# Six wide products per weight block, the softmax epsilon folded into z, and one sum of exponentials per token tile

## The chip, the cores and the metric

The kernel runs on one core of one Trainium2 chip. A core has five engines that run side by side and meet only at semaphores: TensorE (PE) multiplies matrices, VectorE (DVE), ScalarE (ACT) and GpSimd (POOL) work element by element, and SyncE (SP) issues most DMAs. Matrix products land in PSUM, which has eight banks; everything else that is on the chip lies in SBUF. The metric is the device time of one execution in microseconds, lower is better; a profiled execution gives the span and what each engine did in it.

## What is computed

A pre-norm linear attention block followed by a token-mixing MLP, on 2048 tokens of width 512, with 32 heads of 16 and a hidden width of 1792 over the tokens. Cut to what matters:

```python
pq = einsum("bhsd,hdf->bhsf", q, w_phi); pk = einsum("bhsd,hdf->bhsf", k, w_phi)
phi_q = concat([softmax(pq), softmax(-pq)], -1)      # over the 16 features of a head
phi_k = concat([softmax(pk), softmax(-pk)], -1)
kv  = einsum("bhsf,bhsd->bhfd", phi_k, v)
z   = einsum("bhsf->bhf", phi_k)
den = einsum("bhqf,bhf->bhq", phi_q, z)[..., None] + 1e-6
o   = einsum("bhqf,bhfd->bhqd", phi_q, kv) / den
h   = x + concat_heads(o) @ wo                        # x: the input; q, k, v from layernorm(x)
# token mixing, on g = layernorm(layernorm(h))
u   = gelu(einsum("bsd,sf->bdf", g, w1) + b1)         # sums over the tokens
out = h + transpose(einsum("bdf,fs->bds", u, w2) + b2)
```

## The kernel before

All products run on PE in 32-bit form with operands split into a high and a low part: hi x hi, hi x lo and lo x hi are added up in PSUM, three matmuls for one product (`mm3`, or its like with other names).

**Attention.** The 2048 tokens are 16 tiles of 128. K, V and Q are projected tile by tile; the exponentials of a Q tile, for both signs, lie in the tile `eq` (128 x 1024: 64 groups of 16). For the quotient each tile needs the sums of its exponentials for both signs (`smq`, in PSUM, by `q_sum`, line 229), the same sums weighted with z (`ez` = `eq` * `zB` on POOL, line 456, then a sum on DVE into `tz`, line 465), and from both the factor `w` (lines 466 to 471), by which POOL scales `eq` (line 474). The softmax sums of the two signs stand crosswise: `q_sum` writes the sum of sign c to place 1 - c, so that `tz`, multiplied with it, brings the two signs to a common denominator. Line 466 adds the 1e-6 of the reference. `zB`, z summed over all tokens and broadcast to all rows, comes from PE and is copied out by ACT (line 503). From line 432 on the order of PE, DVE, ACT and POOL is that of the code; a loop over `it` (line 716) runs the steps of different tiles side by side, and `turns` (line 175) deals out two lists of DVE operations alternately. Before line 432 a scheduler orders the engines by its own estimates. The normalized tiles `hs` get their low part from POOL (line 62), and the first matrix products of the MLP (`fill`, `pu`) read them.

**The last stage.** `out` is made of eight blocks `sp` of 256 tokens. Each sums over seven slices `p` of the hidden width; a block is a 2 x 2 matrix product computed with seven products of half size instead of eight (operand sums `wraw`, split into `whi` and `wlo`, for the weights; `un` and `uf` for the hidden values). A product takes one of two forms: *wide* (line 1106) is one matmul of 512 columns, hi weights times the high and the low half of the values side by side, and one of 256 columns, lo weights times the high half; the two halves of its PSUM bank are added by the engine that reads it. *narrow* (line 1110) is three matmuls of 256 columns that all add into half a bank, so that two narrow products share a bank. The table `PROD` gives for each product its operands, its bank and, where it is narrow, its half; of the seven, five are wide and two narrow, on six banks. The last block uses the table `LAST`, narrow products alone on four banks. Banks are handed out in turn from all eight, so a block begins on banks that the block before it has not used and goes on to banks that it has.

At the end of a block, its last two slices run product by product, so that banks fill one after the other, and DVE and ACT read them (lines 1162 to 1181): ACT copies one half of bank 0 and the second halves of three banks (`low`), DVE forms the sums `e`, `u2`, `u3` and the outputs `ot`, and POOL issues DMAs that add `ot` and `low` to `out`. Between these, DVE also prepares weights for later steps: for each group of two steps `sums_w2` (lines 857 to 859), `hi_w2` on ACT (line 992) and `lo_w2` (line 1002). Seven slices per block and two per group make blocks alternate: after blocks with an even number a group's `lo`, `hi` and `sums` come within the reading of the banks; in blocks with an odd number `lo`, `hi` and `sums` come at slice 5, ahead of it.

Of the kernel before, what the change touches and what calls it, by code (L numbers as in the profile page):

```python
# [9 lines left out]
F32 = mybir.dt.float32  # L10
# [7 lines left out]
P = 128  # L18
# [6 lines left out]
GRP = 2  # L25
# [5 lines left out]
V_NOT = (0, 1, 11)  # L31
SUMS = 8
LAG = 5
WARM = 9
# [4 lines left out]
def block_kernel(ctx: ExitStack, tc: tile.TileContext, x, xT, wT, phic, wo, w1, b1, w2, b2,  # L39
# [17 lines left out]
    nc.vector.memset(eps2, EPS * EPS)  # L57

# [88 lines left out]
    def signs(e):  # L147
        return e.rearrange("p g (a c h d) -> p (g a) c h d", a=2, c=2, h=2)
# [75 lines left out]
    def q_sum(t):  # L224

        assert t < SUMS or t - SUMS in W, "a tile's sums would go where others are still wanted"
        SQ[t] = sums[:, t % SUMS]
        e = signs(EQ[t])
        return [lambda c=c: nc.vector.reduce_sum(SQ[t][:, :, 1 - c], e[:, :, c], axis=AX.X) for c in range(2)]

# [227 lines left out]
    def s_den(t):  # L458


        tz = az.tile([P, NPR, 2, 2], F32, name="tz")
        den = az.tile([P, NPR, 2], F32, name="den")
        W[t] = az.tile([P, NPR, 2, 2], F32, name="w", bufs=3)
        other = SQ[t]
        return [lambda: nc.vector.reduce_sum(tz.rearrange("p g c h -> p (g c h)"), heads(EZ[t]), axis=AX.X),
                lambda: nc.vector.scalar_tensor_tensor(tz[:, :, 0], other[:, :, 1], 1e-6, tz[:, :, 0],
                                                       op0=ALU.mult, op1=ALU.add),
                lambda: nc.vector.tensor_mul(tz, other, tz),
                lambda: nc.vector.reduce_sum(den, tz.rearrange("p g c h -> p g h c"), axis=AX.X),
                lambda: nc.vector.reciprocal(den, den),  # L470
                lambda: nc.vector.tensor_mul(W[t], other, den.unsqueeze(2).to_broadcast([P, NPR, 2, 2]))]  # L471
# [28 lines left out]
    for g in range(2):  # L500
        pz = ps_k.tile([P, 4, P], F32, name="pk_ps")
        nc.tensor.matmul(pz, ones, zacc[:, 4 * g:4 * g + 4, :], start=True, stop=True)
        nc.scalar.activation(zB[:, 4 * g:4 * g + 4, :], pz, AF.Copy)  # L503
    q_exp(0)
# [94 lines left out]
    def s_moments(t):  # L599

        junk = ak.tile([P, D], F32, name="hj", bufs=1)
        if t == 0:
            ak.tile([P, 104], F32, name="end", bufs=1)
        nc.scalar.activation(VE[t][:, 1:2], VE[t][:, 2:3], AF.Copy, scale=-1.0 / D)
        nc.scalar.activation(junk, HT[t], AF.Square, bias=VE[t][:, 1:2], accum_out=VE[t][:, 3:4])
        nc.scalar.activation(VE[t][:, 0:1], VE[t][:, 3:4], AF.Identity, scale=(1.0 + EPS) / D, bias=eps2)
        if t >= NT - 2:
            nc.scalar.dma_start(out[t * P:(t + 1) * P, :], HT[t])
# [476 lines left out]
    for p in range(NEAR, NP):  # L1085
# [45 lines left out]
    for n, (sp, p) in enumerate(STEPS):  # L1131
        t = 2 * sp
        last = t + 2 == NT
        if n % GRP == 0 and p < NP - 1:
            lo_w2()
            hi_w2()
            sums_w2()
        if p == 0:
            bank = []
            for _ in range(6):  # L1140
                pool = (ps_f, ps_q, ps_b, ps_b)[n_bank % 8 // 2]
                bank.append(pool.tile([P, 2, HD], F32, name="py", tag="pu"))
# [16 lines left out]
        if not last:  # L1159
# [3 lines left out]
            for i in range(3):  # L1163
                nc.scalar.activation(low[:, i], bank[3 + i][:, 1], AF.Copy)
            nc.vector.tensor_add(e[:, 1], bank[0][:, 1], e[:, 1])
            nc.vector.tensor_sub(u2, bank[1][:, 0], e[:, 1])
            nc.vector.tensor_add(u2, bank[1][:, 1], u2)
            nc.vector.tensor_sub(u3, u2, bank[2][:, 0])
            nc.vector.scalar_tensor_tensor(e[:, 0], bank[2][:, 1], -1.0, u2, op0=ALU.mult, op1=ALU.subtract)

            def out_block(i, h, o, add):
                nc.vector.scalar_tensor_tensor(ot[:, i, h], o, b2s[:, t + i:t + i + 1], add, op0=ALU.add, op1=ALU.add)  # L1172

            out_block(0, 0, bank[2][:, 1], u3)
            out_block(0, 1, bank[3][:, 0], u3)
# [79 lines left out]
```

## Time and profile before

| what | value |
|---|---|
| median of 3 runs | 518.52 us (518.47 to 518.72) |
| the profiled execution, its own time | 518.56 us |
| its span | 516.8 us |
| PE busy | 510.9 us (99%), 3595 matmuls |
| DVE / ACT / POOL busy | 445.5 / 296.8 / 245.0 us |
| granted TensorE clock | 1.00 |

The span runs from the first to the last instruction; the 1.8 us between it and the execution's own time lie around it. A busy engine here means that an instruction of it was under way. Matmuls overlap their neighbours, so the cost of one is read from the distance of starts in a run of them and not from its own duration. The list of waits puts idle time of an engine to the instruction that ended it; the chain is followed back from the last instruction to whatever released each step.

### The profile page before, as it was taken

How to read it: one execution, taken by the hardware profiler on the slowest of the kernel's cores; microseconds unless marked ns; L12 is line 12 of the kernel's file. 1: busy time of each engine (PE TensorE's matmuls, PEld its weight loads, DVE VectorE, ACT ScalarE, POOL GpSimd, SP SyncE). 2: the span in 40 equal slices, each digit the busy share in tenths (PEclk: the TensorE clock that was granted, in tenths of full speed). 3: DMA queues.
4: the chain of work that ended last, by engine and by line, in shares of the span. 5: the costliest groups of instructions: out<-in, count | busy, mean ns of one | idle time of the engine just before them, and what ended most of it. 6: DMA issues, size and time to landing. Idle time of an engine off the chain costs nothing.

```text
span 516.8 us, 9476 instructions
## 1 busy us (share of the span) xinstructions
PE 510.9 (99%) x3595; PEld 442.9 (86%) x3595; DVE 445.5 (86%) x789; ACT 296.8 (57%) x494; POOL 245.0 (47%) x188
## 2 busy tenths in 40 slices
PE   9999999999999999999999999999999999999997
PEld 8888888887877778777788899998889999899997
DVE  6893999986799998777796998989989898988985
ACT  6998944434255876668976643457653434434430
POOL 2479799975999999985343200000002212212220
PEclk9999999999999999999999999999999999999999
DMA  8744310000041324334322233374135787677843
GB/s 313 270 127 122 81 53 29 1 1 3 12 154 41 103 84 140 124 124 122 115 89 83 82 105 104 99 245 141 43 123 117 162 192 171 119 162 159 191 50 77
DMA packets 36300, 58.56 MB, mean 113 GB/s; under 512 B 3744, under 2 KB 19360, under 8 KB 36256
## 3 DMA queue, kind: packets, MB, share of 16 engines
q1 hardware_dynamic: 31648, 50.85, 31.3%
q0 software_dynamic: 4032, 6.42, 9.9%
q8 instruction: 28, 0.46, 0.4%
q10 hardware_dynamic: 576, 0.69, 0.4%
q14 instruction: 16, 0.13, 0.1%
HBM read 46.81 MB, written 11.14 MB: 112 GB/s over the span
## 4 chain that ended last, share of the span: by engine, by line
PE 89%; POOL 7%; DVE 2%; ACT 1%; issue 1%; POOLq 0%
PE py L1106 17%; PE pu L936 12%; PE py L1110 10%; PE pu L66 7%; PE pu L67 7%; PE pu L68 7%; PE pv L67 3%; PE pv L68 3%; PE pv L66 3%; PE pk_ps L66 2%; PE pk_ps L68 2%; PE pk_ps L67 2%; POOL ez L456 2%; POOL eq L474 2%; PE po L68 2%; PE tn L548 2%
## 5 line engine op out<-in xcount | busy, mean ns | idle before, releaser
L1176 POOL DMA_DIRECT2D out<-ot x7 | 6.2, 884 | 142.1 <-DVE ot L1172 142.1
L992 ACT ACTIVATE whi<-wraw 128x1792 fp32r<-128x1792 f32 x28 | 47.6, 1701 | 44.1 <-DVE wraw L859 20.3
L1002 DVE TENSOR_TENSOR wlo<-wraw,whi 128x1792 fp32r<-128x1792 f32 x28 | 56.6, 2021 | 8.4 <-PE py L1110 6.9
L67 PE MATMUL pu<-hs,whi 128*128 128x512 f32 x128 | 50.3, 393 | 1.2 <-POOL hs L62 1.2
L66 PE MATMUL pu<-hs,whi 128*128 128x512 f32 x128 | 50.1, 399 | 0.0
L1106 PE MATMUL py<-uf,whi 128*128 128x512 f32 x175 | 48.4, 393 | 0.0
L68 PE MATMUL pu<-hs,wlo 128*128 128x512 f32 x128 | 48.0, 390 | 0.0
L897 ACT ACTIVATE whi<-wraw 128x896 fp32r<-128x896 f32 x24 | 22.9, 954 | 31.2 <-PE pu L936 26.4
L456 POOL TENSOR_TENSOR ez<-eq,zB 128x1024 f32<-128x1024 f32 x16 | 38.3, 2399 | 4.4 <-ACT zB L503 4.4
L1110 PE MATMUL py<-uf,whi 128*128 128x256 f32 x210 | 39.0, 283 | 0.0
L936 PE MATMUL pu<-ht,whi 128*128 128x256 f32 x192 | 35.6, 283 | 0.0
L208 POOL TENSOR_TENSOR pk<-pk,sk 128x1024 f32<-128x1024 f32 x16 | 30.9, 1938 | 7.3 <-DVE sk L207 7.2
L62 POOL TENSOR_TENSOR hs<-hb,hs 128x512 fp32r<-128x512 f32 x16 | 22.4, 1400 | 23.9 <-ACT hs L61 23.8
L550 ACT ACTIVATE pht<-tn 128x512 f32<-128x512 f32 x32 | 17.4, 595 | 28.4 <-PE tn L548 28.3
L474 POOL TENSOR_TENSOR eq<-eq,w 128x1024 f32<-128x1024 f32 x16 | 32.4, 2028 | 1.3 <-DVE w L471 1.2
L1110 PEld LDWEIGHTS py<-uf,whi 128*128 128x128 f32 x210 | 32.7, 192 | 0.0
L1106 PEld LDWEIGHTS py<-uf,whi 128*128 128x128 f32 x175 | 29.8, 189 | 3.5
L212 POOL TENSOR_TENSOR zacc<-zacc,pk 128x1024 f32<-128x1024 f32 x13 | 31.2, 2399 | 0.5
L1106 PEld LDWEIGHTS py<-uf,wlo 128*128 128x128 f32 x175 | 27.9, 190 | 4.0
L66 PEld LDWEIGHTS pu<-hs,whi 128*128 128x128 f32 x128 | 24.1, 188 | 7.2 <-issue 2.5
L936 PEld LDWEIGHTS pu<-ht,whi 128*128 128x128 f32 x192 | 30.0, 192 | 0.0
L1110 PE MATMUL py<-uf,wlo 128*128 128x256 f32 x105 | 29.7, 283 | 0.0
(207 smaller groups left out, 1625.0 us busy)
## 6 DMA issues: line engine op xcount, KB each, us to landing
wraw<-in_w SPq DMA_DIRECT2D x28, 512.0 KB, 4.5
wraw<-in_w SPq DMA_DIRECT2D x48, 256.0 KB, 2.8
xraw<-in_xT SPq DMA_DIRECT2D x16, 256.0 KB, 3.1
xh<-in_x SPq DMA_DIRECT2D x16, 256.0 KB, 2.7
h<-in_x SPq DMA_DIRECT2D x16, 256.0 KB, 2.7
out<-h SPq DMA_DIRECT2D x14, 256.0 KB, 2.7
out<-ot POOLq DMA_DIRECT2D x14, 256.0 KB, 4.8
wraw<-in_wT SPq DMA_DIRECT2D x12, 256.0 KB, 4.6
```

The source lines that it names most:

```text
L66: nc.tensor.matmul(o, ah, bh, start=first, stop=False)
L67: nc.tensor.matmul(o, ah, bl, start=False, stop=False)
L68: nc.tensor.matmul(o, al, bh, start=False, stop=last)
L208: nc.gpsimd.tensor_mul(heads(PK[t]), heads(PK[t]), sk.unsqueeze(2).to_broadcast([P, 2 * H, DH]))
L212: nc.gpsimd.tensor_add(zacc, zacc, PK[t])
L456: nc.gpsimd.tensor_mul(EZ[t], EQ[t], zB)
L474: nc.gpsimd.tensor_mul(heads(EQ[t]), heads(EQ[t]), W[t].rearrange("p g c h -> p (g c h)").unsqueeze(2).to_broadcast([P, 2 * H, DH]))
L936: nc.tensor.matmul(ACC[p][bk][:, half], WS[p, i][x][:, a], hb[b][y], start=i == 0 and half == 0 and k == 0, stop=i == NT // 2 - 1 and k == ...
L992: nc.scalar.activation(WH[g], RAW[g], AF.Copy)
L1002: nc.vector.tensor_sub(wl_, RAW[g], WH[g])
L1106: nc.tensor.matmul(o, w, u, start=p == 0 and not low, stop=p == NP - 1, skip_group_check=True)
L1110: nc.tensor.matmul(bank[bk][:, half], AW[sp, p][x][:, a], UB[p, b][:, y], start=p == 0 and half == 0 and i == 0, stop=p == NP - 1 and i == ...
```

## The change

Three things are edited. First, the sums of a tile's exponentials are one DVE reduction over all 64 groups of 16, in their own order, in place of two over 32 groups each; where `w` and the denominator are formed, the result is read with the axis of the signs turned (`[:, :, ::-1]`). Second, line 466 goes: half of 1e-6 is added to each entry of `zB` when ACT copies it out, by an Identity with a bias tile in place of a Copy; summed against the exponentials and multiplied crosswise, the two halves make the same 1e-6. Third, product (0, 0) becomes wide and gets a bank of its own; seven banks are used by blocks 0 to 6 and four by the last. DVE reads one more half bank per block. In the first block the product on the seventh bank is left for slices 0 and 1 together. The sums that odd blocks formed at slice 5 move behind the reading of the banks; after even blocks `lo` and `hi` move behind the last output, but for block 6, where they keep their place.

```diff
+DEN_EPS = 1e-6
...
-    eps2 = cst.tile([P, 1], F32, name="eps2")
+    eps2 = cst.tile([P, 2], F32, name="eps2")
...
-    nc.vector.memset(eps2, EPS * EPS)
+    nc.vector.memset(eps2[:, :1], EPS * EPS)
+    nc.vector.memset(eps2[:, 1:], DEN_EPS / 2)
...
         SQ[t] = sums[:, t % SUMS]
-        e = signs(EQ[t])
-        return [lambda c=c: nc.vector.reduce_sum(SQ[t][:, :, 1 - c], e[:, :, c], axis=AX.X) for c in range(2)]
+        return [lambda: nc.vector.reduce_sum(SQ[t].rearrange("p g c h -> p (g c h)"), heads(EQ[t]), axis=AX.X)]
...
-        other = SQ[t]
+        other = SQ[t][:, :, ::-1]
         return [lambda: nc.vector.reduce_sum(tz.rearrange("p g c h -> p (g c h)"), heads(EZ[t]), axis=AX.X),
-                lambda: nc.vector.scalar_tensor_tensor(tz[:, :, 0], other[:, :, 1], 1e-6, tz[:, :, 0],
-                                                       op0=ALU.mult, op1=ALU.add),
                 lambda: nc.vector.tensor_mul(tz, other, tz),
...
-        nc.scalar.activation(zB[:, 4 * g:4 * g + 4, :], pz, AF.Copy)
+        nc.scalar.activation(zB[:, 4 * g:4 * g + 4, :], pz, AF.Identity, bias=eps2[:, 1:])
...
-    PROD = ((2, 1, 0, None), (5, 5, 1, None), (0, 0, 2, 0), (1, 4, 2, 1), (3, 6, 3, None), (6, 2, 4, None),
-            (4, 3, 5, None))
+    PROD = ((2, 1, 0, None), (5, 5, 1, None), (0, 0, 2, None), (1, 4, 3, 0), (3, 6, 4, None), (6, 2, 5, None),
+            (4, 3, 6, None))
...
         if n % GRP == 0 and p < NP - 1:
             lo_w2()
             hi_w2()
-            sums_w2()
+            if p < NP - 2 or last:
+                sums_w2()
         if p == 0:
             bank = []
-            for _ in range(6):
+            for _ in range(4 if last else 7):
...
         if p == 0:
-            products(sp, [p], order)
+            products(sp, [p], order[:-1] if n == 0 else order)
+            continue
+        if n == 1:
+            steps(sp, [p], order[:-1])
+            products(sp, [0, p], order[-1:])
             continue
...
             nc.vector.tensor_sub(u3, u2, bank[2][:, 0])
-            nc.vector.scalar_tensor_tensor(e[:, 0], bank[2][:, 1], -1.0, u2, op0=ALU.mult, op1=ALU.subtract)
+            nc.vector.tensor_sub(u3, u3, bank[2][:, 1])
+            nc.vector.scalar_tensor_tensor(e[:, 0], bank[3][:, 0], -1.0, u2, op0=ALU.mult, op1=ALU.subtract)
...
             nc.gpsimd.dma_start(out[t * P:(t + 1) * P, :], flat(ot[:, 0]), accum_op=ALU.add)
-            if n % GRP == 0:
+            ahead = t + 4 == NT
+            if ahead:
                 lo_w2()
                 hi_w2()
-            out_block(1, 0, bank[4][:, 0], e[:, 0])
-            out_block(1, 1, bank[5][:, 0], e[:, 1])
+            out_block(1, 0, bank[5][:, 0], e[:, 0])
+            out_block(1, 1, bank[6][:, 0], e[:, 1])
+            if n % GRP == 0 and not ahead:
+                lo_w2()
+                hi_w2()
...
-            if n % GRP == 0:
-                sums_w2()
+            sums_w2()
             continue
```

On PE, in slices 2 and 3 of block 1, where a run of wide matmuls (line 1106, in the new kernel 1105) meets the narrow ones (1110, now 1109), there stood before (a name with a number is one buffer of its kind):

```order
L1106 MATMUL py<-uf,whi 128x512 x10
L1106 MATMUL py<-uf,wlo_4674 128x256 x5
L1110 MATMUL py<-uf,whi 128x256 x2
L1110 MATMUL py<-uf,wlo_4674 128x256
L1110 MATMUL py<-uf,whi 128x256 x2
L1110 MATMUL py<-uf,wlo_4674 128x256
L1106 MATMUL py<-uf,wlo_4674 128x256 x5
```

And now, at the same place on PE:

```order
L1105 MATMUL py<-uf,whi 128x512 x12
L1105 MATMUL py<-uf,wlo_4638 128x256 x6
L1109 MATMUL py<-uf,whi 128x256 x2
L1109 MATMUL py<-uf,wlo_4638 128x256
L1105 MATMUL py<-uf,wlo_4638 128x256 x6
```

One group of three narrow matmuls per slice is gone, and one 512-column and one 256-column matmul per slice have come in its place.

On DVE, at the end of block 1 (an odd one), the reading of the banks stood between these rows before; `u` with a number is `u2` or `u3`:

```order
L1002 TENSOR_TENSOR wlo_4756<-wraw,whi 128x1792
L857 TENSOR_TENSOR wraw<-wraw 128x512
L858 TENSOR_TENSOR wraw<-wraw 128x256
L859 TENSOR_TENSOR wraw<-wraw 128x256
L1165 TENSOR_TENSOR e<-py,e 128x256
L1166 TENSOR_TENSOR u_4798<-py,e 128x256
L1167 TENSOR_TENSOR u_4798<-py,u_4798 128x256
L1168 TENSOR_TENSOR u_4799<-u_4798,py 128x256
L1169 SCALAR_TENSOR_TENSOR e<-py,u_4798 128x256
L1172 SCALAR_TENSOR_TENSOR ot<-py,b2s,u_4799 128x256 x2
L1172 SCALAR_TENSOR_TENSOR ot<-py,b2s,e 128x256 x2
L1002 TENSOR_TENSOR wlo<-wraw_4719,whi 128x1792
```

And now (lines shifted by one to five):

```order
L1001 TENSOR_TENSOR wlo_4716<-wraw,whi 128x1792
L1169 TENSOR_TENSOR e<-py,e 128x256
L1170 TENSOR_TENSOR u_4751<-py,e 128x256
L1171 TENSOR_TENSOR u_4751<-py,u_4751 128x256
L1172 TENSOR_TENSOR u_4752<-u_4751,py 128x256
L1173 TENSOR_TENSOR u_4752<-u_4752,py 128x256
L1174 SCALAR_TENSOR_TENSOR e<-py,u_4751 128x256
L1177 SCALAR_TENSOR_TENSOR ot<-py,b2s,u_4752 128x256 x2
L1177 SCALAR_TENSOR_TENSOR ot<-py,b2s,e 128x256 x2
L856 TENSOR_TENSOR wraw<-wraw 128x512
L857 TENSOR_TENSOR wraw<-wraw 128x256
L858 TENSOR_TENSOR wraw<-wraw 128x256
```

The three operations of `sums_w2` moved from ahead of the nine reading operations to behind them, and these have become ten.

On DVE, in pass 1 of the loop over `it`, where the logits and sums of one tile are dealt out against the denominator of another, there stood before:

```order
L164 TENSOR_REDUCE mx<-pu 128x32
L465 TENSOR_REDUCE tz<-ez 128x64
L165 TENSOR_REDUCE mn<-pu 128x32
L466 SCALAR_TENSOR_TENSOR tz<-smq,tz 128x16x2
L158 TENSOR_TENSOR eq<-pu,mx 128x16x32
L468 TENSOR_TENSOR tz<-smq,tz 128x64
L229 TENSOR_REDUCE smq<-eq 128x16x2
L469 TENSOR_REDUCE den<-tz 128x32
L229 TENSOR_REDUCE smq<-eq 128x16x2
L470 RECIPROCAL den<-den 128x32
L471 TENSOR_TENSOR w<-smq,den 128x64
```

And now:

```order
L166 TENSOR_REDUCE mx<-pu 128x32
L466 TENSOR_REDUCE tz<-ez 128x64
L167 TENSOR_REDUCE mn<-pu 128x32
L467 TENSOR_TENSOR tz<-smq,tz 128x64
L160 TENSOR_TENSOR eq<-pu,mx 128x16x32
L468 TENSOR_REDUCE den<-tz 128x32
L230 TENSOR_REDUCE smq<-eq 128x64
L469 RECIPROCAL den<-den 128x32
L470 TENSOR_TENSOR w<-smq,den 128x64
```

Two operations fewer stand ahead of `w`, and the sum of exponentials is one of double length that stands before the reciprocal.

More of the change, by code (lines that the diff above doesn't have):

```diff
@@ L605, in s_moments @@
         nc.scalar.activation(junk, HT[t], AF.Square, bias=VE[t][:, 1:2], accum_out=VE[t][:, 3:4])
-        nc.scalar.activation(VE[t][:, 0:1], VE[t][:, 3:4], AF.Identity, scale=(1.0 + EPS) / D, bias=eps2)
+        nc.scalar.activation(VE[t][:, 0:1], VE[t][:, 3:4], AF.Identity, scale=(1.0 + EPS) / D, bias=eps2[:, :1])
         if t >= NT - 2:
@@ L1163, in block_kernel @@
             for i in range(3):
-                nc.scalar.activation(low[:, i], bank[3 + i][:, 1], AF.Copy)
+                nc.scalar.activation(low[:, i], bank[4 + i][:, 1], AF.Copy)
             nc.vector.tensor_add(e[:, 1], bank[0][:, 1], e[:, 1])
@@ L1168, in block_kernel @@
             nc.vector.tensor_sub(u3, u2, bank[2][:, 0])
-            nc.vector.scalar_tensor_tensor(e[:, 0], bank[2][:, 1], -1.0, u2, op0=ALU.mult, op1=ALU.subtract)
+            nc.vector.tensor_sub(u3, u3, bank[2][:, 1])
+            nc.vector.scalar_tensor_tensor(e[:, 0], bank[3][:, 0], -1.0, u2, op0=ALU.mult, op1=ALU.subtract)
             def out_block(i, h, o, add):
                 nc.vector.scalar_tensor_tensor(ot[:, i, h], o, b2s[:, t + i:t + i + 1], add, op0=ALU.add, op1=ALU.add)
-            out_block(0, 0, bank[2][:, 1], u3)
-            out_block(0, 1, bank[3][:, 0], u3)
+            out_block(0, 0, bank[3][:, 0], u3)
+            out_block(0, 1, bank[4][:, 0], u3)
             nc.gpsimd.dma_start(out[t * P:(t + 1) * P, :], flat(ot[:, 0]), accum_op=ALU.add)
-            if n % GRP == 0:
+            ahead = t + 4 == NT
+            if ahead:
                 lo_w2()
                 hi_w2()
-            out_block(1, 0, bank[4][:, 0], e[:, 0])
-            out_block(1, 1, bank[5][:, 0], e[:, 1])
+            out_block(1, 0, bank[5][:, 0], e[:, 0])
[3 more added lines that the diff above has]
+                hi_w2()
             nc.gpsimd.dma_start(out[(t + 1) * P:(t + 2) * P, :], flat(ot[:, 1]), accum_op=ALU.add)
```

## The prediction

> **What bounds the kernel.** I read the busy times first, then what PE waits for, then the chain, and then the order of time at three places: the ends of blocks, the attention loop and the start of the last stage. First the page's row of PE, PE's waits (engine, line, releaser: us in total, times, longest), and two stretches of the windows view:
>
> ```profile
> PE 510.9 (99%) x3595; PEld 442.9 (86%) x3595; DVE 445.5 (86%) x789; ACT 296.8 (57%) x494; POOL 245.0 (47%) x188
> ...
> PE pu L67 <- POOL hs L62: 1.2, 1, 1.2
> PE pk_ps L301 <- DVE eps L57: 1.1, 1, 1.1
> PE pk_ps L137 <- ACT wkh L293: 0.2, 1, 0.2
> ...
> 64.00:128.00 64.00, 64.00 (x518) 52.29 (x517) 58.26 (x92) 26.75 (x35) 54.13 (x31) 1.00 0.06 18
> 320.00:380.00 60.00, 60.00 (x407) 55.67 (x406) 55.68 (x120) 34.75 (x52) 0.00 (x0) 1.00 0.42 132
> ```
>
> PE is a wall. In 516.8 us it shows three waits, and only one in the body of the program: 1.2 us for POOL. So the change can gain what it takes out of PE's own queue plus at most that wait, and it can lose wherever PE newly waits. The rows of a kernel whose DVE is busy 86% invite one to count DVE operations; those are worth nothing here unless PE was waiting for them.
>
> **What a product costs on PE.** From the chain in order of time (start, us, what) and the timeline of PE (start, us, then idle time if any); the rows from 399.67 on are a run of two slices:
>
> ```profile
> 388.91 1.44 PE py L1110 x12
> 407.59 2.78 PE py L1106 x16
> 475.15 1.44 PE py L1110 x12
> 495.94 17.64 PE py L1110 x147
> ...
> 399.67 2.46 PE L1106 MATMUL py<-uf,whi 128*128 128x512 f32 x10
> 401.96 0.76 PE L1106 MATMUL py<-uf,wlo 128*128 128x256 f32 x5
> 402.56 0.40 PE L1110 MATMUL py<-uf,whi 128*128 128x256 f32 x2
> ...
> 409.52 0.40 PE L1106 MATMUL py<-un,whi 128*128 128x512 f32 x1
> 411.64 0.40 PE L1106 MATMUL py<-un,whi 128*128 128x512 f32 x1
> ```
>
> The last block, narrow products alone, takes 17.64 us for 147 matmuls: 0.120 us each, so a narrow product is 3 x 0.120 = 0.360 us. Ten matmuls of 512 columns take 401.96 - 399.67 = 2.29 us, 0.229 each, and five of 256 columns 402.56 - 401.96 = 0.60, again 0.120: a wide product is 0.349 us. Run product by product, eight wide ones (x16) take 2.78 us, 0.3475 each. The columns are the same, 768; one instruction fewer saves 0.011 to 0.0125 us. These prices make a block 7 x (5 x 0.349 + 2 x 0.360) = 17.26 us, and the same twelve matmuls come back every (475.15 - 388.91) / 5 = 17.25 us, so nothing else lies in a block. The exchange is made in 7 blocks x 7 slices = 49 products: 0.54 to 0.61 us; I take **0.55 us**.
>
> The Trainium skill, "TensorE: Matmul & The Clock Gate", section "Back-to-back issue gap", gives an isolated matmul N/2.4 ns plus a fixed 2.5 ns at full clock. By that, one matmul fewer would be worth 2.5 ns, 49 of them 0.12 us, and the time 518.4. The trace disagrees: its 256-column matmul stands 120 ns apart where the rule has 109, and the measurement decides.
>
> **The banks.** Seven of eight banks per block leave one free one for the next block. Let T be the first matmul of the next block, 409.52. By the prices above, bank 0 of the ending block is complete at T - 4.2, banks 1 to 5 at T - 3.5, - 2.8, - 2.1, - 1.4, - 0.7, bank 6 at T. The next block needs old bank 0 at T + 0.35, 1 at 0.70, 2 at 1.05, 3 at 1.40, 4 at 1.75, 5 at 2.10. Before, its sixth product needs old bank 3 at 411.64. DVE and ACT at this (odd) end, and DVE at the even end after it:
>
> ```profile
> 406.34 0.36 ACT L1162 ACTIVATE e<-py 128x256 f32<-128x256 f32 x1
> ...
> 404.87 2.03 DVE L1002 TENSOR_TENSOR wlo<-wraw,whi 128x1792 fp32r<-128x1792 f32 x1 [1.26 <-PE py L1110]
> 408.33 0.42 DVE L1165 TENSOR_TENSOR e<-py,e 128x256 f32<-128x256 f32 x1
> 409.84 0.42 DVE L1168 TENSOR_TENSOR u<-u,py 128x256 f32<-128x256 f32 x1
> 410.52 0.87 DVE L1172 SCALAR_TENSOR_TENSOR ot<-py,b2s,u 128x256 f32<-128x256 f32 x2
> 411.30 0.87 DVE L1172 SCALAR_TENSOR_TENSOR ot<-py,b2s,e 128x256 f32<-128x256 f32 x2
> ...
> 423.17 0.42 DVE L1165 TENSOR_TENSOR e<-py,e 128x256 f32<-128x256 f32 x1
> 426.87 2.03 DVE L1002 TENSOR_TENSOR wlo<-wraw,whi 128x1792 fp32r<-128x1792 f32 x1 [0.38 <-PE py L1106]
> ```
>
> Before, the pair of outputs at 410.52 ends at 411.39 and frees bank 3 a quarter of a microsecond ahead of its use at 411.64. That was the tightest hand-over, and PE did not wait. Now the sums have left their place, and DVE can begin right behind `wlo`, at 406.8, T - 2.7 (the copy by ACT is done at 406.70). At the pitch of the rows (408.33 to 409.84 for three operations), the new subtraction 0.46 behind L1168, bank 0 is free at T - 2.3, 1 at - 1.3, 2 at - 0.3, 3 at + 0.4, 4 at + 0.8, 5 at + 1.2: the least margin is 0.9 us. At even ends DVE begins at 423.17, T - 3.6, and all six are free by T + 0.4. So **no wait for banks: 0**, and the tenth reading operation (0.42 us, the row of L1168) lies under PE. If that cover were gone, it would cost 0.42 us at an end.
>
> What is late instead: behind odd ends the sums now start at about T + 1.6, and the next `lo` ends about T + 5.1 (before, sums and `lo` were done by T + 4.6). PE's first lo matmul on it stands in slice 2: two slices (4.89) and twelve 512-column matmuls (2.75) behind T, at T + 7.6, a margin of 2.5 us. Behind even ends `lo` ends at T + 2.6, needed at slice 1's end of hi matmuls, T + 5.2. At block 6 `lo` keeps its place and waits for PE as at 426.87. In the POOL queue, after even ends, the second `ot` DMA now stands ahead of the first `low`; nothing on PE reads `out`.
>
> **The start of the last stage.** Bank 6 of block 0 is a bank that the last hidden slice has just filled, read by the activation:
>
> ```profile
> 377.26 1.37 ACT L800 ACTIVATE u<-pu,b1s 128x512 f32<-128x512 f32 x2 [4.72 <-PE pu L68]
> ...
> 377.74 1.07 PE L1106 MATMUL py<-un,whi 128*128 128x512 f32 x4
> ```
>
> It is the first of the two tiles, read by 377.95. PE reaches the product on it after what is left of slice 1, two hi, six small wide and three narrow matmuls, 1.4 us behind 377.74: 0. The scheduler also reorders some matmuls before 126 us and among the fills around 365 us; the windows above have PE at 64.00 of 64 and 60.00 of 60, with its inputs ready: 0, bounded at 0.3 either way, about PE's one short wait in such a place (0.2).
>
> **The attention loop.** DVE's groups (x count, busy, mean ns), then DVE, POOL and PE in order of time:
>
> ```profile
> L229 DVE TENSOR_REDUCE smq<-eq 128x32 f32<-128x512 f32 x32 | 21.9, 683 | 0.2
> L465 DVE TENSOR_REDUCE tz<-ez 128x64 f32<-128x1024 f32 x16 | 19.3, 1209 | 3.9 <-POOL ez L456 3.9
> L466 DVE SCALAR_TENSOR_TENSOR tz<-smq,tz 128x32 f32<-128x32 f32 x16 | 3.0, 187 | 0.3
> ...
> 185.66 1.38 DVE L665 TENSOR_TENSOR wlo<-wraw,whi 128x512 fp32r<-128x512 f32 x1
> 191.28 2.22 DVE L665 TENSOR_TENSOR wlo<-wraw,whi 128x512 fp32r<-128x512 f32 x1
> ...
> 164.70 0.55 POOL L611 TENSOR_TENSOR r<-ve,mhalf 128x1 f32<-128x1 f32 x1 [0.67 <-ACT ve L606]
> 166.56 2.39 POOL L474 TENSOR_TENSOR eq<-eq,w 128x1024 f32<-128x1024 f32 x1
> 174.38 2.39 POOL L474 TENSOR_TENSOR eq<-eq,w 128x1024 f32<-128x1024 f32 x1
> 179.09 1.29 POOL L62 TENSOR_TENSOR hs<-hb,hs 128x512 fp32r<-128x512 f32 x1
> 182.20 1.94 POOL L474 TENSOR_TENSOR eq<-eq,w 128x1024 f32<-128x1024 f32 x1
> 184.10 2.40 POOL L456 TENSOR_TENSOR ez<-eq,zB 128x1024 f32<-128x1024 f32 x1
> 186.44 1.74 POOL L62 TENSOR_TENSOR hs<-hb,hs 128x512 fp32r<-128x512 f32 x1
> ...
> 188.23 0.50 PE pu L67
> ```
>
> No row has a sum of 1024 values into PSUM; L465 has the input, L229 the output, and between them it costs 1.21 to 1.37 us; I take 1.21, since length sets these. A tile then saves 2 x 0.683 - 1.209 + 0.187 = 0.34 us of DVE. A read with the signs turned has no row; the nearest is L466, which takes every other pair of the same PSUM tile in 0.187. I add nothing; were the two such reads of a tile each slower by that much, 0.37, the tile would come out even. Sixteen tiles: 5.5 us of DVE, and `w` comes 0.3 us earlier.
>
> Is that on PE's path? The one wait ends at 188.2, when POOL's `hs` is done. Back from there POOL works without a gap (no row on the way shows idle time) to 164.70, where it waits for ACT, which follows PE; `w`, needed at 166.56, 174.38 and 182.20, is not what it waits for. An earlier `w` only lies longer. So **the 1.2 us stay: 0**.
>
> The epsilon: an Identity with a bias has no row of this size without a scale; L503's copy is the floor, L624's Identity with scale and bias the ceiling:
>
> ```profile
> 127.92 0.60 ACT L503 ACTIVATE zB<-pk_ps 128x512 f32<-128x512 f32 x1 [0.26 <-PE pk_ps L502]
> 168.44 0.82 ACT L624 ACTIVATE hb<-h,ve,r 128x512 f32<-128x512 f32 x1
> ```
>
> That is 0 to 0.22 us each, 0.44 for two, on POOL's start into `ez` at 128.5; POOL's wait of 0.67 at 164.70 takes it up: 0. The second small memset delays nothing: PE's first matmul waits for `ones` alone, ahead of it.
>
> **Sum.** 518.56 (this execution; the median is 518.52) - 0.55 + 0 = **518.0 us**. On its own this case spans 517.5 to 518.6: 0.61 and 0.3 below, 0.3 above with half the gain lost. From no change, a measurement of this kernel can tell about 0.2%, 1.04 us; this lies within.
>
> **Rivals.** *Faster: POOL reaches `hs` earlier.* Two of the scalings of `eq` take 2.39 us where the third takes 1.94, and `hs` takes 1.74 where the one before it has 1.29; each time DVE's L665 runs at that boundary. That is 0.45 + 0.45 + 0.45 = 1.35 us ahead of PE's wait. If the shift of DVE by 0.3 us moves these out, the wait goes: 518.0 - 1.2 = **516.8**. Against it: at 191.28 L665 took 2.22 us because `ez` was running, so it gets in when a POOL operation ends, wherever in it it came; at 185.66 it would have to come 1.6 us earlier to miss `ez` of 184.10. One collision gone is worth 0.45, which brings 517.55, at the edge. Chance 0.26.
>
> *Slower: the banks come too late at odd ends.* Should DVE begin there as before, at T - 1.2, then by the same pitches bank 3 is free at T + 1.95 against 1.40 needed, 0.55 late, and the next bank adds 0.1: 0.65 for each of blocks 1, 3 and 5, 2.0 us, **520.0**. It decides once DVE begins later than T - 1.8 (0.9 of margin gone). For it: the hand-over was within 0.25 us before, with one bank less in use. Against it: the sums stand behind the reading now. Chance 0.12.
>
> *The wide form gains nothing*, as the 512-column matmul's distance grows behind a sixth: then 518.5, within 0.2% too.
>
> **Chances.** Within 0.2%: 0.62 (the sum with its own range, and the wide form without gain). Faster 0.26, slower 0.12. The range leaves out the slower rival and the outer part of the faster one: 516.6 to 519.0.
>
> **What would show it.** Right: 49 matmuls fewer; the twelve narrow matmuls of a pair of slices now six, and block to block 17.18 us; no PE wait on DVE or ACT with `py`; PE's wait on `hs` still 0.8 to 1.6 us; the new `smq` group x16 near 1.2 us; L466's group gone. Wrong: a wait of `py` on DVE at odd ends; an `hs` wait that is gone, or one grown beyond 2 us; a `smq` sum far over 1.4 us.

## The result, and the profile after

The changed kernel takes 517.23 us, median of 10 runs (516.99 to 517.78), against 518.50 us for the kernel before in the same comparison: a ratio of 0.9979 with a 95% interval of 0.9971 to 0.9987. The forecast was 518.0 in a range of 516.6 to 519.0. Sign and mechanism held, the size did not: 1.27 us where 0.55 had been worked out. Where the other 0.7 us are from is what the experiments are about.

The page's row of the engines' busy time in the profile after, and then PE's waits there (engine, line, releaser: us in total, times, longest):

```profile
PE 509.3 (99%) x3546; PEld 439.3 (85%) x3546; DVE 445.9 (87%) x765; ACT 297.2 (58%) x494; POOL 244.6 (47%) x188
```

```profile
PE pu L69 <- POOL hs L64: 1.2, 1, 1.2
PE pk_ps L302 <- DVE eps L59: 1.1, 1, 1.1
PE pk_ps L139 <- ACT wkh L294: 0.2, 1, 0.2
PE po L70 <- DVE ol L577: 0.2, 1, 0.2
```

3595 - 3546 = 49 matmuls are gone. No wait of `py` has come, and the 1.2 us for POOL's `hs` stay. A wait of 0.2 us for `ol` in the attention loop is new; of the runs below, e_wide has it with before's attention code and a_split lacks it with after's, so it does not go with the edits there.

Where the time went is best read from four rows of the chain of waits (start, us, what), which appear in every profile of this study: the first full product of keys, the sum of z behind the projections, the fills of the hidden layer, the last block. First of before, then of after:

```profile
10.44 2.62 PE pk_ps L137 x16
126.17 1.72 PE pk_ps L502 x4
292.80 60.47 PE pu L936 x504
...
492.41 1.44 PE py L1110 x12
```

```profile
9.74 2.61 PE pk_ps L139 x16
125.44 1.72 PE pk_ps L501 x4
292.05 60.47 PE pu L935 x504
...
388.71 0.71 PE py L1109 x6
...
423.00 0.71 PE py L1109 x6
440.14 0.71 PE py L1109 x6
...
491.57 0.71 PE py L1109 x6
...
494.37 17.64 PE py L1109 x147
```

With the last block of before at 495.94 (in the prediction), the difference is 0.70 us at the first product, 0.73 at z, 0.75 at the fills and 1.57 at the last block. So the gain is made in two places: 0.70 us in the first ten microseconds, where the change adds only a second small memset, which the prediction put at nothing, and 203.14 - 202.32 = 0.82 us in the stage of the products. Between them, in projections and attention, it is 0.05. The block-to-block time is 440.14 - 423.00 = 17.14 us, where 17.18 had been forecast and 17.25 stood before. From the first to the last of these rows, over six blocks, it is 491.57 - 388.71 = 102.86 us against 492.41 - 388.91 = 103.50 before (388.91 is in the prediction): 0.64 us for 42 exchanges. The other 0.18 of the 0.82 us belong to the fills and the first block (block 1 begins 99.48 us behind the first of the fills before, and 99.30 now); one block's share by the 0.64 would be 0.11.

DVE at the same odd end that the prediction took, in after (T, the first matmul of the next block, is 408.49):

```profile
403.87 2.03 DVE L1001 TENSOR_TENSOR wlo<-wraw,whi 128x1792 fp32r<-128x1792 f32 x1 [1.06 <-PE py L1109]
405.81 0.42 DVE L1169 TENSOR_TENSOR e<-py,e 128x256 f32<-128x256 f32 x1
407.78 0.42 DVE L1173 TENSOR_TENSOR u<-u,py 128x256 f32<-128x256 f32 x1
410.02 0.68 DVE L856 TENSOR_TENSOR wraw<-wraw 128x512 f32<-128x512 f32 x1
411.54 2.02 DVE L1001 TENSOR_TENSOR wlo<-wraw,whi 128x1792 fp32r<-128x1792 f32 x1
```

DVE starts reading right behind `wlo`, at T - 2.7; the reading operation that is new (L1173) takes 0.42; the sums start at T + 1.5 and the next `lo` ends at T + 5.1: each within 0.1 us of its step in the prediction.

The attention loop of after: the two sums of a tile, then DVE, POOL and PE around PE's wait, in order of time.

```profile
L466 DVE TENSOR_REDUCE tz<-ez 128x64 f32<-128x1024 f32 x16 | 19.4, 1209 | 4.0 <-POOL ez L457 4.0
L230 DVE TENSOR_REDUCE smq<-eq 128x64 f32<-128x1024 f32 x16 | 19.3, 1204 | 0.0
L467 DVE TENSOR_TENSOR tz<-smq,tz 128x64 f32<-128x64 f32 x16 | 3.5, 220 | 0.3
```

```profile
184.40 1.92 DVE L664 TENSOR_TENSOR wlo<-wraw,whi 128x512 fp32r<-128x512 f32 x1
...
183.39 2.38 POOL L457 TENSOR_TENSOR ez<-eq,zB 128x1024 f32<-128x1024 f32 x1
185.73 1.72 POOL L64 TENSOR_TENSOR hs<-hb,hs 128x512 fp32r<-128x512 f32 x1
...
187.50 0.50 PE L69 MATMUL pu<-hs,whi 128*128 128x512 f32 x1 [1.15 <-POOL hs L64]
```

The sum of 1024 values into PSUM costs 1204 ns, as the one into SBUF does (1209), and the product that reads it with the signs turned costs 220. DVE got ahead here: its `wlo` starts 0.55 us earlier against POOL's `hs` than before (185.73 - 184.40 = 1.33, where it was 186.44 - 185.66 = 0.78). It then took 1.92 us instead of 1.38, ended 0.6 us into `hs` as before, and `hs` took its 1.72 us again.

### The profile page after: what moved, and what is told of

It is laid out like the page before. It is cut to its first block, busy times and chain, and to the rows that moved or that the text cites. A ratio compares the mean times of both kernels' runs of the same rounds, so it can differ in the third digit from the quotient of the medians.

```text
span 515.2 us, 9360 instructions
## 1 busy us (share of the span) xinstructions
PE 509.3 (99%) x3546; PEld 439.3 (85%) x3546; DVE 445.9 (87%) x765; ACT 297.2 (58%) x494; POOL 244.6 (47%) x188
## 4 chain that ended last, share of the span: by engine, by line
PE 94%; POOL 3%; ACT 1%; DVE 1%; issue 0%; POOLq 0%
PE py L1105 20%; PE pu L935 12%; PE pu L68 8%; PE pu L69 8%; PE pu L70 8%; PE py L1109 7%; PE pv L69 3%; PE pv L70 3%; PE pv L68 3%; PE pk_ps L68 3%; PE pk_ps L69 2%; PE pk_ps L70 2%; PE tn L547 2%; PE po L70 2%; PE po L69 2%; PE po L68 2%
## 5 line engine op out<-in xcount | busy, mean ns | idle before, releaser
L1105 PE MATMUL py<-uf,whi 128*128 128x512 f32 x210 | 57.6, 393 | 0.0
L1105 PEld LDWEIGHTS py<-uf,whi 128*128 128x128 f32 x210 | 35.8, 189 | 4.3
L1105 PEld LDWEIGHTS py<-uf,wlo 128*128 128x128 f32 x210 | 33.1, 190 | 4.6
L1105 PE MATMUL py<-uf,wlo 128*128 128x256 f32 x210 | 34.9, 280 | 0.0
L186 ACT ACTIVATE pk<-pk,r 128x1024 f32<-128x1024 f32 x16 | 18.3, 1146 | 21.1 <-DVE pk L164 21.1
L68 PEld LDWEIGHTS pu<-hs,whi 128*128 128x128 f32 x128 | 24.0, 188 | 7.1 <-issue 2.5
L69 PEld LDWEIGHTS pu<-hs,whi 128*128 128x128 f32 x128 | 24.1, 188 | 6.6 <-POOL hs L64 2.1
```

Source lines behind the costliest of these rows:

```text
L68: nc.tensor.matmul(o, ah, bh, start=first, stop=False)
L69: nc.tensor.matmul(o, ah, bl, start=False, stop=False)
L1105: nc.tensor.matmul(o, w, u, start=p == 0 and not low, stop=p == NP - 1, skip_group_check=True)
```

## The experiments

All fourteen profiles can be laid against each other by the four rows of the chain. The columns are the start of the first product of keys, and the three stages between the rows, in us; before and after stand first.

| kernel | first product | to z | attention, to the fills | fills and products, to the last block | median of runs |
|---|---|---|---|---|---|
| before | 10.44 | 115.73 | 166.63 | 203.14 | 518.50 |
| after | 9.74 | 115.70 | 166.61 | 202.32 | 517.23 |
| before_again | 10.27 | 115.73 | 166.62 | 203.14 | 518.00 |
| e_attn | 10.19 | 115.70 | 166.69 | 203.09 | 518.16 |
| e_wide | 10.08 | 115.71 | 166.66 | 202.30 | 517.44 |
| a_split | 10.58 | 115.71 | 166.69 | 205.84 | 520.79 |
| a_split1 | 10.62 | 115.70 | 166.67 | 202.97 | 517.79 |
| a_lo128 | 10.25 | 115.72 | 166.60 | 200.27 | 515.25 |
| a_sums_early | 10.43 | 115.71 | 166.61 | 204.76 | 520.17 |
| a_hs2_dve | 9.62 | 115.72 | 166.54 | 202.30 | 517.22 |
| a_neg15 | 9.94 | 115.76 | 165.92 | 202.32 | 516.69 |
| b_neg15 | 10.17 | 115.70 | 165.88 | 203.11 | 517.34 |
| a_neg14 | 10.90 | 115.75 | 166.77 | 202.45 | 517.84 |
| a_cold | 12.37 | 116.17 | 166.65 | 202.30 | 519.41 |

The medians are of several comparisons, each with its own runs of before; the ratios below stand against those. A stage with the same code and order of matmuls repeats within 0.1 us; the first column does not. Two rows stand out, where the order differs from after's: a_cold in the projections (116.17), a_neg14 among the fills (202.45). That makes it possible to tell apart effects that the medians, whose runs spread over 0.5 us and more, cannot.

**Is the start-up's 0.70 us the change's?** The kernel before, once more, unchanged.

> The kernel before, unchanged, profiled and timed once more. In the first profile of before the matmuls of the first 6.7 us stand 213 ns apart and then 112 ns; in the profile of after the step comes at 5.2 us, and that alone is 0.70 us of the two profiles' difference. Theory A (the moment of the step is chance of the execution, not of the code): the step falls somewhere else again, between about 4.5 and 8 us, the ratio's interval holds 1.000, and the runs spread over some 0.8 us as before. Theory B (the change moved the step): the step is again at 6.7 us.

The ratio is 0.9999 (0.9990 to 1.0008). The fold, which multiplies `w_phi` into the projections' weights, in after and in before (rows of PE in order of time), then two stretches of before (PE busy and its matmuls, PEld, DVE, ACT, POOL, granted clock, DMA):

```profile
5.24 2.02 PE L282 MATMUL pu<-ph,wraw 128*128 128x128 f32 x16
```

```profile
5.19 2.78 PE L281 MATMUL pu<-ph,wraw 128*128 128x128 f32 x16
```

```profile
6.00:7.00 1.00, 1.00 (x7) 1.00 (x7) 0.86 (x3) 0.68 (x2) 0.00 (x0) 1.00 1.06 390
7.00:8.00 1.00, 1.00 (x11) 1.00 (x10) 0.69 (x1) 0.97 (x3) 0.00 (x0) 1.00 1.06 366
```

The same 16 matmuls take 2.02 us in after and 2.78 in before: by their single starts they stand 213 ns apart until 6.7 us in before, until 5.2 in after, and 112 ns from there on (the two stretches of before show 7 matmuls under way in a microsecond, then 11). The granted clock reads 1.00 in both (the column behind POOL's), so only the matmuls' distance tells it. In the repeat of before the step came at 6.5 us, in other profiles between 4.0 and 7.1. The repeat alone, with 6.5 us beside 6.7, does not tell the theories apart; the others do. The first product starts between 9.62 and 10.90 us in the eleven other profiles, with the second memset at both ends of that span, and all of the change that acts so early is in e_attn below, whose ratio is 0.9997. Theory A holds: it was chance. Nor does the second memset delay PE: after's list of waits names it, as the last before PE's first matmul, but that starts at 1.06 us in before and in after:

```profile
1.06 4.21 PE L301 MATMUL pk_ps<-ones 128*128 128x128 f32 x18 [1.06 <-DVE eps L57]
```

```profile
0.97 0.06 DVE L59 MEMSET eps<- 128x1 f32 x1
1.06 4.14 PE L302 MATMUL pk_ps<-ones 128*128 128x128 f32 x18 [1.06 <-DVE eps L59]
```

The spread is not the step alone: where it came at 4.0 us, in e_attn, PE then waited 0.8 us for the weights' centering.

The Trainium skill, "TensorE: Matmul & The Clock Gate", section "Part 1: The HAM clock gate", describes such a step: matmuls at half rate until PE has been busy for some 3.4 us, by a window that runs on its own and does not start with the kernel. The trace agrees on the ratio (213 to 112 ns) and on a moment that moves, but by more than the 0.5 us either way that the section names: 4.0 to 7.1 us here. The next run tests the rest of it.

**What sets the step.**

```diff
-WARM = 9
+WARM = 1
```

> After, with 1 instead of 9 warming products of ones by ones at the start. In the profiles so far the matmuls' distance falls from 213 to 112 ns between 2.9 and 6.0 us behind the first one, at no fixed time. Theory A (the step needs PE to have been busy for some microseconds, and falls by chance within such a stretch): the fold that begins at 5.2 us now runs its first 3 to 6 us at 213 ns, the step comes at 8 to 11 us, the first product of keys starts 1 to 2.5 us later, 518.2 to 519.7. Theory B (the step comes by the time since the start alone): at 4 to 7 us as before, 517.2.

519.41 us, a ratio of 1.0024 (1.0013 to 1.0035), within theory A. PE's rows of the folds:

```profile
5.22 3.75 PE L282 MATMUL pu<-ph,wraw 128*128 128x128 f32 x16 [3.37 <-DVE wraw L272]
8.77 2.91 PE L282 MATMUL pv<-ph,wraw 128*128 128x128 f32 x16
```

They show the first fold at the slow distance throughout (16 matmuls in 3.75 us), the step comes at 10.85 us, 5.6 us behind the fold's start, and the first product 2.6 us later than in after. Theory B falls. The eight warming products save about 2 us (519.41 - 517.23 = 2.2); the step's scatter stays, and it is most of the spread in the table's first column.

**Which edit brings the rest?** Each half of the change alone: the sixth wide product with its banks (e_wide), and the sums, the epsilon and the memset (e_attn).

> Before with the third edit alone: the sixth wide product, the seven banks and the epilogue; sums, epsilon and memsets as before. Theory A (all of the gain is the exchange of 49 products, at 0.011 to 0.0125 us each by the prediction, at up to 0.017 by the two profiles): 517.7 to 518.0, 0.55 to 0.85 us under before, block to block 17.14 to 17.18 us. Theory B (the attention edits bring the 0.7 us of the start-up): the same block to block, but at least 0.4 us above after, near 518.0, and the start-up step at 6.7 us. A rule of 2.5 ns a matmul: 0.12 us.

> Before with the first two edits alone: one sum a tile with the signs' axis turned, 1e-6 spread over z, the second memset; five wide products as before. Theory A: no change, 518.3 to 518.7 and a ratio whose interval holds 1.000, although DVE has some 5 us less to do; PE still waits 1.1 to 1.2 us for hs. Theory B: 0.4 to 0.7 us faster, with the start-up step near 5.2 us.

e_wide: 0.9986 (0.9977 to 0.9994), with 202.30 us in the products' stage, as in after. e_attn: 0.9997 (0.9988 to 1.0005), with 166.69 in the attention and 203.09 behind it, as in before. The wide product brings the 0.82 us of the stage; DVE's saved time brings nothing.

**The price of a matmul.** After, with the 512-column matmul of all six wide products cut into two of 256 columns:

```diff
+        if sp == NT // 2 - 1 or low:
             nc.tensor.matmul(o, w, u, start=p == 0 and not low, ...)
+            return
+        for i in range(2):
+            nc.tensor.matmul(o[:, i], w, u[:, i], start=p == 0 and i == 0, ...)
```

> After, with the 512-column matmul of each wide product in the first seven blocks issued as two of 256 columns into the same bank: 6 x 7 x 7 = 294 matmuls more, the columns, the banks, the readings and the other engines unchanged. It is the price of one matmul more, six times over. By the prediction's rows (0.011 to 0.0125 us each): 3.2 to 3.7 us above after, 520.4 to 520.9. By the two profiles' stage (0.0153 to 0.017 each): 4.5 to 5.0 above, 521.7 to 522.2. By 2.5 ns each: 0.74 above, 518.0.

205.84 - 202.32 = 3.52 us for 294 matmuls: 0.0120 us each, within the prediction's rows; 520.79 us, a ratio of 1.0053 (1.0040 to 1.0065). The 2.5 ns of the rule that the prediction cites are excluded. But with the 49 exchanges between before and after the stage is 0.82 us shorter, 0.0167 for each; by the six blocks alone, free of fills, it is 0.64 / 42 = 0.0152. So the sixth wide product was worth more than an average one: from all split to before, five wide ones gained (205.84 - 203.14) / 245 = 0.0110 each, just the lower price of the prediction (0.360 - 0.349).

To see what a matmul waits for, the low matmuls of the wide products were halved in columns.

```diff
+        k = HD if sp == NT // 2 - 1 else HD // 2
-        o, u = (bank[bk][:, 0], u[:, 0]) if low else (bank[bk], u)
+        o, u = (bank[bk][:, 0, :k], u[:, 0, :k]) if low else (bank[bk], u)
```

> After, with the low matmul of each wide product in the first seven blocks taken over 128 instead of 256 columns (half of the low weights' part is left out): 294 matmuls lose 128 columns, and no instruction goes. Theory A (between 256-column matmuls PE waits for its weight loads, which come every 0.120 us whatever the columns): runs of such matmuls stay at 0.120 us, and the time falls by less than 3 us, from matmuls that stand behind a 512-column one. Theory B (the columns set the distance, at 0.43 ns a column as between 256 and 512): 0.055 us less each, 16 us, 501.

202.32 - 200.27 = 2.05 us, 515.25 us in all (ratio 0.9939, 0.9927 to 0.9952). Theory A is near: most of 16 us of columns were worth nothing. Not in every word: behind the first 128-column matmul that follows a 512-column one, the next comes after 59 ns, but a 512-column one behind short ones then takes 285 ns instead of 231; and in a run of 128 columns they stand 111 ns apart, not 120.

```profile
410.06 0.22 PE L1106 MATMUL py<-un,wlo 128*128 128x128 f32 x1
410.12 0.45 PE L1106 MATMUL py<-un,whi 128*128 128x512 f32 x1
410.41 0.22 PE L1106 MATMUL py<-un,wlo 128*128 128x128 f32 x1
410.46 0.45 PE L1106 MATMUL py<-un,whi 128*128 128x512 f32 x1
```

The windows view of four stretches of 20 us from 400 to 480 us (PE, PEld, DVE and on), its sums for before_again and for a_split:

```profile
sum 80.00, PE 80.00 PEld 73.06 DVE 71.66 ACT 35.21 POOL 14.74; mean PE 20.00 PEld 18.27 DVE 17.91 ACT 8.80 POOL 3.68
```

```profile
sum 80.00, PE 80.00 PEld 80.00 DVE 71.72 ACT 33.44 POOL 14.69; mean PE 20.00 PEld 20.00 DVE 17.93 ACT 8.36 POOL 3.67
```

With 256-column matmuls alone the weight loads are busy in all of the 80 us; with five wide products in 73.06. I take from both runs that loads, not columns, set the distance of short matmuls here. That columns do not is shown by a_lo128; that loads do is argued, since the rows of loads overlap (192 ns each in the narrow group of before's page, at a distance of 120) and are busy all the time by that alone, and no run takes a load away by itself. The last run on prices asked whether the extra price lies in short matmuls that follow each other: one product, (3, 6), split, which stands among 512-column ones in four of seven slices (the line is that of the kernel with all six split).

```diff
-        if sp == NT // 2 - 1 or low:
+        if sp == NT // 2 - 1 or low or (a, b) != (3, 6):
```

> After, with the 512-column matmul of one wide product only (the fifth in the row, (3, 6)) issued as two of 256 columns: 49 matmuls more, as many as before had more than after, but the extra ones stand among 512-column matmuls in four of seven slices, and not behind other 256-column ones. Measured so far from the chain: 49 exchanges between before and after are worth 0.82 us in the stage from the fills to the last block, 294 in the split of all six 3.52, 0.0120 each. Theory A (each matmul more has its price wherever it stands): 0.5 to 0.85 us more in that stage, 517.8 to 518.0 with after's start-up. Theory B (only 256-column matmuls that follow one another run up against the weight loads at 0.120 us; behind a 512-column one they stand 0.113 to 0.118 apart): 0 to 0.3 us more, 517.2 to 517.5.

202.97 - 202.32 = 0.65 us, 0.0133 each, and the same by six blocks of this run, 493.13 - 389.71 = 103.42 against 102.86:

```profile
389.71 0.71 PE py L1113 x6
...
493.13 0.71 PE py L1113 x6
```

Theory B falls: in the three arrangements a matmul more costs 0.012 to 0.015 us in the blocks. Why the pair of narrow products of before costs 0.17 us more than this arrangement of the same count, 0.08 of it in these six blocks (103.50 - 103.42), stays open.

**The slower rival.** The sums of the next slab put back ahead of the reading:

```diff
-            if p < NP - 2 or last:
-                sums_w2()
+            sums_w2()
...
-            sums_w2()
+            if n % GRP == 0:
+                sums_w2()
```

> After, with the sums of the next slab put back where before had them: at odd block ends ahead of DVE's reading of the banks. The prediction's rival (the banks come too late at odd ends): DVE begins there at T - 1.2 instead of T - 2.7, bank 3 is 0.55 us late and the next one 0.1 more, 0.65 us for each of blocks 1, 3 and 5, about 2.0 us above after: 519.2, with PE waits of py on DVE in those three places and in no other. Other theory: the hand-over has more room than I worked out, and the place of the sums is worth nothing: 517.2, no such wait.

520.17 us (1.0032, 1.0019 to 1.0044), and 204.76 - 202.32 = 2.44 us in the stage. DVE at the odd end (T is 409.20), PE there, and the whole of what the list of waits has of all three odd ends:

```profile
406.52 0.69 DVE L856 TENSOR_TENSOR wraw<-wraw 128x512 f32<-128x512 f32 x1
408.04 0.42 DVE L1168 TENSOR_TENSOR e<-py,e 128x256 f32<-128x256 f32 x1
410.01 0.42 DVE L1172 TENSOR_TENSOR u<-u,py 128x256 f32<-128x256 f32 x1
```

```profile
410.12 0.28 PE L1105 MATMUL py<-un,wlo 128*128 128x256 f32 x1
410.57 0.48 PE L1109 MATMUL py<-un,whi 128*128 128x256 f32 x2 [0.17 <-DVE u L1172]
410.89 0.28 PE L1109 MATMUL py<-un,wlo 128*128 128x256 f32 x1
411.21 0.50 PE L1105 MATMUL py<-un,whi 128*128 128x512 f32 x1
```

```profile
PE py L1109 <- DVE u L1172: 0.5, 3, 0.2
```

DVE starts at T - 1.2, and PE loses 0.8 us at each of the three odd ends. The first bank to come late is old bank 2, which the added subtraction (L1172 here) frees, not bank 3. The list of waits shows 0.5 of 2.44 us: PE's rows overlap, and a hand-over that comes late by less than a matmul's length, here 410.89 to 411.21, leaves next to no idle time there. A missing wait in that list does not prove a gapless engine; the distances of the matmuls and the stage's length do.

**The faster rival.** It held that PE's 1.2 us go if POOL comes earlier. POOL was relieved of `hs` of tile 2 itself (a_hs2_dve), and then of 1.3 us of other work, the second sign of one tile's logits: the last tile's in after (a_neg15) and in before (b_neg15), and in after that of the tile ahead of it (a_neg14, with 14 for 15).

```diff
-        split(HN[t][:, 0], HN[t][:, 1], hn, nc.gpsimd)
+        split(HN[t][:, 0], HN[t][:, 1], hn, nc.vector if t == 2 else nc.gpsimd)
```

```diff
-            return logit_ops(PS[n], EQ[n], n >= len(Q_AT))
+            return logit_ops(PS[n], EQ[n], n >= len(Q_AT) and n != 15)
```

> After, with the subtraction that makes the low half of hs of tile 2, the one PE waits 1.2 us for, done by DVE instead of POOL. Theory A (PE is a wall with one gap in it, and the gap is POOL's lateness): the wait is gone and 1.1 to 1.2 us with it, 516.0 to 516.2. Theory B (POOL or DVE makes PE wait for something else a little later): the wait moves, 517.0 or more.

> After, with the second sign of the last token tile's logits made by DVE (0.68 us, from PSUM) instead of by POOL (0.25 + 1.06 us): POOL has 1.3 us less to do just ahead of the hs that PE waits for, DVE 0.68 us more. Theory A (the attention edits freed DVE time that is worth nothing where it lies, but can be spent on POOL's lateness): hs comes 1.3 us earlier, the stage with PE's wait is 0.4 to 1.2 us shorter than in after, 516.1 to 516.8 with after's start-up. Theory B (DVE, then late with the low weights, makes PE wait as long, as with tile 2's hs on DVE): the stage is within 0.2 us of after's, 517.2.

> Before, with the same move of the last tile's second sign from POOL to DVE. Theory A: DVE has some 0.3 us a tile less room than in after, so the low weights come late in the place of hs: the stage with PE's wait is at most 0.3 us shorter than in before, 518.2 to 518.6. Theory B (the attention edits have no part in it): before gains or fails to gain in that stage as much as after does.

> After, with the second sign of the last tile but one moved from POOL to DVE: the same exchange one tile earlier, so that DVE's 0.68 us more lie 8 us ahead of PE's wait and not just before it. Theory A: hs 1.3 us earlier and DVE recovered by then, PE's wait gone, 516.0 to 516.3 with after's start-up. Theory B: as for the last tile, 517.2, or a new wait for the exponentials of that tile.

PE's waits in a_hs2_dve, then in a_neg15:

```profile
PE pu L70 <- DVE wlo L664: 0.8, 2, 0.4
```

```profile
PE pu L70 <- DVE wlo L664: 0.4, 1, 0.4
```

With `hs` on DVE the wait for POOL is gone, but two for DVE's low weights take its place: 166.54 us in the stage, 0.07 less than after, and 517.22 us. Theory B. With the last tile's sign moved one wait remains: 165.92, 0.69 less, and 516.69 us, a ratio of 0.9973 (0.9964 to 0.9983): below before, while against after only the stage tells it, as the two intervals overlap. One tile earlier (a_neg14) the same move makes the stage 0.16 longer, and the median is 517.84: the wait for `hs` is gone there too, but PE falls 0.5 us behind after's pace in the products ahead of it and waits 0.4 us for `wlo` behind it. And before gains as much by it as after does: 166.63 - 165.88 = 0.75, 517.34 us, a ratio of 0.9985 (0.9976 to 0.9994). So my theory that DVE's time, freed by the sums, pays for this move falls; the room was there before.

## Why the prediction was right and wrong

- **PE is a wall, and 49 matmuls are the gain.** Right: e_wide has the whole of the stage's gain, e_attn none of it.
- **The price of an exchange, 0.011 to 0.0125 us.** This is the step that failed. The term measured 0.82 us instead of 0.55: 0.0152 an exchange in the blocks, 0.75 for 49, and 0.07 more ahead of the second block, where the fills' order also moves and no run parts the two. The prediction subtracted mean distances of groups; these are not constants of a form. Over two blocks, the high matmuls' distance falls from 231.7 to 231.2 ns and that of the narrow ones from 119.7 to 119.0 as their neighbours change. At before's means the 14 exchanges of two blocks are worth 14 x (3 x 119.7 - 231.7 - 117.5) = 0.14 us; 34.50 - 34.29 = 0.21 were measured. As a price of an average matmul the reading was good (0.0120 over 294). Why the neighbours change the distances stays open.
- **The rule of 2.5 ns a matmul** (the Trainium skill, "TensorE: Matmul & The Clock Gate", section "Back-to-back issue gap"), set aside for the trace: rightly; it would make 0.74 us of the 3.52.
- **Banks, 0.** Right, at the odd end with its times within 0.1 us. At the even end of block 2, where T is 425.63, the next `lo` ended at T + 3.0 and not at T + 2.6, with 2.2 us still in hand. The rival's mechanism is real and was priced at 2.0 for a measured 2.44; it named bank 3 as the first late one, which was bank 2. Its own pitches had that: 1.5 us later than T - 0.3 is T + 1.2, for T + 1.05.
- **Start of the last stage and the fills, 0, bounded at 0.3.** Right within the bound: the 0.07 us above are all that the blocks' pace leaves over, and a_neg14, with another order of the fills, has 0.13 in the same place. The stages ahead of it repeat within 0.1 us.
- **Attention, 0.** Right: DVE's operations cost what was taken (1.204 for 1.21 us), and the 1.2 us stay. Also right was the reason, that DVE's low-weight operation gets in at the end of a POOL operation, wherever in it it came. One number of the sum did not come: DVE's busy time was to fall by 5.5 us there and rise by 2.9 at the blocks' ends, and it is 445.9 after 445.5. The sums and line 466 did save 5.6; but the 18 low-weight operations of the attention loop took 19.7 us instead of 17.6 (one is the row at 184.40, 1.92 for 1.38); the last 1.0 us is not accounted for. DVE's busy time holds such waiting, and is no measure of the work saved.
- **The faster rival's price, 1.2 us for the wait.** Wrong even as a rival: take POOL's lateness away, and the stage is between 0.69 us shorter and 0.16 longer, since DVE is next.
- **What the sum lacked** is a term for the start. The sum was made against one execution, whose first product came at 10.44 us, late among those seen. The 0.3 us above and the 0.61 below did not have this scatter in them. Of the 1.27 us between the medians, 0.82 to 0.84 are shown as the change's (the stage in both profiles of the wide form, after and e_wide); the rest is within the medians' interval of 0.7 to 1.5 us, and no run shows it as the change's.
- **Range and chances.** Here there was luck. The sum's own span of 517.5 to 518.6 (its terms make 517.6 of the lower end) did not hold 517.23; the stated range did, by the room below that was left for the faster rival, which did not come. The ratio of 0.9979 also lies just beyond the 0.2% that got the chance of 0.62; the 0.82 us that are shown are 0.16%.
- **Two readings.** Old bank 3 was needed at 411.64 by the seventh product, on the sixth bank, and not by the sixth product. That PE's first matmul waits for `ones` alone is not what the list says, which names `eps`; that the second memset costs nothing is shown by the start at 1.06 us.

## What to carry to other kernels

Lay two profiles against each other by the same few rows of the chain before explaining a difference: here stages of 100 to 200 us repeat within 0.1 us, while the first ten microseconds differ by up to 1.3 us with hardly a change in their code. Read the price of one instruction more or less from a pair of stretches that differ in nothing else, not from two groups' means. Saved time on an engine beside a wall was worth nothing here, and PE's one wait was worth only the distance to the engine that was late next.

## What the runs showed of the hardware

- The first matmuls of 128 columns stand at 1.9 times the later distance (213 and 112 ns), until between 4.0 and 7.1 us with nine warming products and until 10.85 us with one, while the granted clock reads 1.00. One warming product instead of nine cost 2.2 us; with nine the first product of keys still starts anywhere between 9.62 and 10.90 us.
- Halving the columns of 294 matmuls from 256 to 128 took off 2.05 us, 7 ns each, where 128 columns are worth 55 ns by the distances of 256 and 512. Among 512-column matmuls the time only moves on: 59 + 285 ns where 115 + 231 stood.
- The same columns in one matmul fewer were worth 11 to 15 ns in the blocks, by what stood around it (0.0110, 0.0120, 0.0133 and 0.0152 us).
- A sum of 1024 values costs the same into PSUM (1204 ns) as into SBUF (1209), and turning the signs' axis in the reading of PSUM leaves a product of 64 values at 220 ns.
- DVE's two-input operation on SBUF took 0.68 to 2.50 us in the same loop, by how much of a POOL operation was left when it came; the POOL operation behind it took 1.72 us instead of 1.29.
